# Summing the inverse steps' products in float32, wider layernorm statistics, integer table angles, and a new instruction order in a one-core Hyena-style convolution and gMLP kernel

## The chip, the core and the metric

One core of a Trainium2 chip runs the whole kernel. The time is the device time of one execution in microseconds; lower is better. Engines are named as in the profile: PE (TensorE matmul), PEld (its weight loads), DVE (VectorE), ACT (ScalarE), POOL (GpSimd) and SP (SyncE, which issues most DMAs).

## What is computed

The reference, cut to what matters (S = 2048, D = 640, F = 1728, batch 1, bfloat16 in and out):

```python
mod = (_silu(c) @ w_mod).reshape(1, 6, 1, -1)
sa, ca, ga, sb, cb, gb = ...
h = _layernorm(x) * (1 + ca) + sa
x = x + ga * _A_ref(h, A_k, A_v, A_shift_k, A_ssm_k, A_ssm_D)
h = _layernorm(x) * (1 + cb) + sb
x = x + gb * _B_ref(h, B_w_in, B_w_sp, B_b_sp, B_w_out)

def _A_ref(q, k, v, shift_k, ssm_k, ssm_D):
    kv = short_conv4(k, shift_k) * v
    y = irfft(rfft(pad(kv)) * rfft(pad(ssm_k)))[:S]      # along S
    return q * (y + kv * ssm_D)

def _B_ref(x, w_in, w_sp, b_sp, w_out):
    z = _gelu(x @ w_in)
    z1, z2 = z[..., :Fh], _layernorm(z[..., Fh:])
    g = einsum('ts,bsf->btf', w_sp, z2) + b_sp
    return (z1 * g) @ w_out
```

## The kernel before

The kernel has three stages, and one list of numbered operations covers the first two.

**The convolution stage** makes the long convolution by a Fourier transform that is written as matmuls. The 640 channels are cut into 5 units of 128 channels. For each unit, a short convolution on PE (`taps`) and a product with v on DVE (`tv`) give kv, which goes through DRAM and comes back in another layout (`kvw`, `ldX`). For the filter K and for kv (U) alike, `stage1` makes 4 groups of 4 matmuls, each evicted by `s1c`; then 8 forward steps (`forward`, 6 matmuls each) give the transform in 2 blocks of frequencies per step. A step of K is kept as bfloat16 by ACT (`khc`, the tile KH). A step of U is handled by `u_item`: DVE multiplies the real and imaginary parts from PSUM with KH, four products at a time (`prod`, 1024 elements per partition); PE transforms back (`inv`), and `zc` evicts the result into the unit's tile Z. There are 5 x 8 = 40 such items. `MODE` gives each a letter. With `u` the four products are stored in bfloat16 (tag T) and PE sums them as it transforms: 12 matmuls per item. With `s` the products are stored in float32 (tag Tf); two operations `csum` on POOL or DVE (256 elements each) form the real and imaginary sums (tile W), and PE needs 6 matmuls. Before, each unit has the letters `susussus`: 25 items are summed, 15 are not. Units 0 to 3 turn Z by a DMA transpose (`zt`) and finish with `y` on PE and `ym` on DVE; unit 4 turns on PE (`zfl`, `zk`, `yl`, `yml`). `ghm` multiplies and adds the modulation vectors, and `res` adds each unit to x.

**Tables.** The transform's cosines are made at the start (`m2_base`, `m2_chunk`): angles in float32 turns, reduced by adding and subtracting a large constant (`turns`, `msub`, on DVE), then a sine on ACT (`msin`). `msgn`, `mneg`, `gcopy` and `gneg` fill the signed and transposed copies M2 and G2.

**Statistics of the second layernorm.** In `resid`, DVE takes `bn_stats` (`ln2`) of each 128-row tile of x in three pieces: units 0 and 1 together (256 channels), units 2 and 3 together (256), and unit 4 (128). `ag2` joins the pieces, `rstd2` on POOL and `nmr2` on DVE make scale and shift, and `zx` normalises.

**The z stage** works in 4 groups of 4 row tiles. Group 0 is turned on PE (`hfl`, `hmod`); groups 1 to 3 are turned by a DMA transpose (`turn`) and modulated in place (`hmod2` on DVE, ACT or POOL). Then 16 products with `w_in` per group (`zz`, 5 matmuls of 432 columns each), `gelu` on ACT, statistics of the z2 half (`stz`, `agz`, `rstdz`, `nmrz`) and its normalisation (`zn`).

**The last stage** mixes along the sequence and projects out, both with a blocked product of 7 multiplications instead of 8 (lines 1012 and 1178). It is written out by hand, and is not touched by the change.

**What sets the order.** `ORDER` is a list of engine letters with operation numbers, written out in full; `Plan.run` issues the operations in that order, and each engine works through its own in that order. So every move between engines and every change of place is in that list. `FILLS` gives the counts of matmuls of 512 columns on a constant tile (`fill`), which compute nothing that is used; before there are three, all near the start. `SLOTS` gives the number of buffers for each tag.

Lines in the profile: L244 is the matmul helper of the first two stages, L247 the copy helper (`s1c`, `khc`, `zc`, `zk`, `gcopy`), L461 `prod`, L475 `csum`, L342 `turns`, L344 `msub`, L347 `msin`, L352 `msgn`, L607 and L609 `xn`, L660 `ghm`, L677 `ym`, L697 `res`, L703 `ln2`, L745 `yml`, L828 `ag2`, L832 `nmr2`, L844 `zx` on POOL, L857 `hfl`, L870 `hmod`, L888 `turn`, L896 `hmod2`, L925 `stz`.

Of the kernel before, what the change touches and what calls it, by code (L numbers as in the profile page):

```python
# [21 lines left out]
MAGIC = 12582912.0  # L22
# [11 lines left out]
FILLS = (9, 3, 6, )  # L34
MODE = ('susussus', 'susussus', 'susussus', 'susussus', 'susussus')
SLOTS = dict(Tf=2, W=2, X=3, X1=4, KH=9, T=3, Z=3, ZT=1, wm=1, big=2, dg=2, st1=2, s1=1, sm=2, pu=2, pz=2)
# [4 lines left out]
D0 G101 S524 D100 D102 S19 D103 S82 S2 A4 G5 S20 D121 A1 D104 D18 D109 D13 D14 P1032 P7 A105 S83 D110 D127 G6 A531 D10  # L41
S21 D15 A16 P1033 P8 D23 D11 A106 A112 S22 A111 D86 S88 D122 P26 D17 D115 A532 D87 A123 S523 D36 A533 D116 P145 A124 S3
A118 P24 P154 A117 A146 D147 D125 D27 D25 G119 A155 P1034 P151 D107 S34 D113 G126 P30 D153 G114 D31 A156 A152 G120 P28
P148 A534 A149 P133 D29 D90 D150 A134 P227 A108 P142 P161 D527 S32 P136 S33 A162 S35 D143 D528 P167 S84 P157 A228 A168
S85 P233 P171 A158 P139 P159 A234 D137 A172 P39 S526 D529 A128 D140 D530 P41 A160 P229 P163 D535 D40 A164 G536 S46 P43
G141 P173 A230 D42 P182 G48 A174 D44 D537 D184 P37 A175 A183 P179 P176 P9 A181 P231 A177 D38 P169 D178 P165 D180 S45
A170 G138 G135 P185 D542 G144 A166 D186 P195 A549 D196 G187 A232 P49 G188 A12 G553 S47 P201 P53 P211 D202 A543 G197
D212 P189 G198 S89 P217 D218 P203 P235 S525 G130 A544 A190 A204 G213 D54 P199 P205 P251 A236 G214 P191 D50 G72 G554
A252 S91 S565 P219 S58 P253 D206 A220 P249 A250 D192 A254 D200 P51 P239 D538 P221 A240 P193 D555 G131 G207 P257 A545
D222 D52 A258 D539 D540 S59 P247 A248 P215 P55 P255 P568 A256 A569 P245 D56 D541 D93 A246 P237 A238 G223 D546 G60 G224  # L50
G208 P566 A567 A550 G547 S57 P259 P265 P301 D260 D551 P61 D194 P241 D548 S570 A302 A216 P307 G557 P209 D266 A308 S92
P67 A242 P305 S94 A306 G561 P291 D68 D62 D292 P295 G562 P225 P303 D296 P573 G558 A556 G261 P243 D574 P571 S575 A559
# [30 lines left out]
D897 D1009 S1041 D1002 A993 D962 D965 P944 D991 P1024 A945 D1059 D1050 D987 S1040 D963 A898 A1025 A964 P1018 P958 D896  # L83
D994 P948 D995 A1019 D988 P1020 G1026 P1067 D1063 A959 D1027 A1021 D1057 D1029 A1028 D1060 D1061 P1012 A1030 D1031
D1064 P1069 A1013 A1068 D1062 D1058 P1071 D1072 D1065 A1070 A949 P1078 D1066 P1074 D1075 D1043 P1073 D1079 D1076 P1010
P1022 P1080 P1016 A1011 S1077 D1081 A1023 A1017 S1082
"""


# [39 lines left out]
def kernel(  # L129
# [80 lines left out]
    with ExitStack() as pctx:  # L210
# [482 lines left out]
        def resid(u, g, ns):  # L693
# [5 lines left out]
            if u not in (1, 3, 4):  # L699
                return  # L700
# [602 lines left out]
```

## Time and profile before

| | us |
|---|---|
| median of 3 runs | 307.67 |
| lowest and highest of them | 307.53, 308.72 |
| the profiled execution, its own time | 308.43 |
| its span, from first to last instruction | 306.6 |
| PE busy | 294.8 |
| DVE busy | 272.8 |
| ACT busy | 162.0 |
| POOL busy | 140.8 |

The span holds 6479 instructions at a mean granted TensorE clock of 0.988. Busy times are averages over stages with different limits, so they are read stage by stage. A matmul counts as busy from its issue to its modelled end, and matmuls overlap; the time that a series holds PE is read from the chain of waits, not from the mean duration of one. A group's busy time divided by its count leaves out the overlap of neighbours on DVE, so it lies a little below the mean duration shown beside it.

### The profile page before, as it was taken

The numbers are of one execution on the slowest core, as the hardware profiler recorded it, in microseconds if no ns is written. First come the engines' busy times: TensorE is split into PE (matmuls) and PEld (weight loads), VectorE is DVE, ScalarE is ACT, GpSimd is POOL, SyncE is SP. The second block draws the span as 40 slices with busy tenths as digits, with TensorE's granted clock in tenths as the row PEclk, the third lists the DMA queues.
The fourth block names the chain that finished last, engine by engine and source line by source line (L and its number), as shares of the span: only waits on it lengthen the run. The fifth ranks groups of instructions, "written<-read, shape, count | busy, mean of one in ns | idle before, by whom it ended". The sixth has DMA issues, their size and how long they took to land.

```text
span 306.6 us, 6479 instructions
## 1 busy us (share of the span) xinstructions
PE 294.8 (96%) x2482; PEld 195.9 (64%) x2482; DVE 272.8 (89%) x567; ACT 162.0 (53%) x287; POOL 140.8 (46%) x175
## 2 busy tenths in 40 slices
PE   6899999999999999799999999999999999999996
PEld 2476787888799888655555455555555656565554
DVE  7998999999999999979848999989989889898675
ACT  5996989998578855557656758320211111021110
POOL 2217858659796878782627231000513214040412
PEclk9799999999999999979999999999999999999999
DMA  8999999999483969205897930036758594630324
GB/s 180 227 263 249 248 255 273 227 223 238 136 203 79 219 194 274 71 3 101 199 135 169 162 53 0 0 62 137 143 116 191 80 181 91 164 81 21 83 45 123
DMA packets 127955, 45.23 MB, mean 148 GB/s; under 512 B 117071, under 2 KB 127156, under 8 KB 127924
## 3 DMA queue, kind: packets, MB, share of 16 engines
q1 hardware_dynamic: 127770, 44.78, 67.0%
q8 instruction: 19, 0.31, 0.4%
q14 instruction: 12, 0.10, 0.1%
q10 hardware_dynamic: 154, 0.05, 0.1%
HBM read 16.11 MB, written 5.24 MB: 70 GB/s over the span
## 4 chain that ended last, share of the span: by engine, by line
PE 76%; DVE 14%; DMA 4%; issue 2%; POOL 1%; ACT 1%; SPq 1%; DVEq 0%; POOLq 0%
PE ps L1012 22%; PE pu L244 17%; PE pz L244 13%; PE po L1178 7%; PE sm L244 7%; PE s L244 4%; DMA ZT<-Z 3%; PE pz L1012 2%; DVE Tf L461 2%; DMA KH<-in_A_ssm_D_dram 2%; DVE stz L925 1%; PE pu L1012 1%; DVE gh L677 1%; PE po L1139 1%; DVE st L703 1%
## 5 line engine op out<-in xcount | busy, mean ns | idle before, releaser
L244 PEld LDWEIGHTS <-Z 128*128 128x128 bf16 x320 | 31.5, 99 | 29.3 <-issue 2.2
L244 PE MATMUL pu<-X,M 128*128 128x128 bf16 (+1 forms) x480 | 45.8, 237 | 0.7 <-ACT KH L247 0.2
L1199 POOL TENSOR_TENSOR O<-O,xt 128x320 f32<-128x320 f32 x7 | 6.6, 946 | 84.8 <-ACT O L1198 84.8
L244 PEld LDWEIGHTS <-M 128*128 128x128 bf16 x480 | 37.8, 98 | 6.2 <-issue 1.5
L1012 PEld LDWEIGHTS <-S 128*128 128x128 bf16 x256 | 25.0, 98 | 21.2
L475 POOL TENSOR_TENSOR W<-Tf 128x256 bf16<-128x256 f32 x44 | 32.0, 744 | 13.4 <-DVE Tf L461 8.0
L244 PE MATMUL pu<-big,Z 128*128 128x432 bf16 x160 | 34.4, 358 | 0.9 <-DVE Z L896 0.8
L247 ACT CAST X<-s 128x1024 bf16<-128x1024 f32 x31 | 31.5, 1017 | 7.0 <-PE s L244 6.9
L244 PE MATMUL pz<-big,Z 128*128 128x432 bf16 x160 | 32.9, 347 | 0.0
L1196 ACT COPY O<-po 128x320 f32<-128x320 f32 x7 | 3.0, 425 | 52.9 <-PE po L1178 52.9
L461 DVE TENSOR_TENSOR Tf<-pu,KH 128x1024 f32<-128x1024 f32 x25 | 30.2, 1216 | 0.6 <-ACT KH L247 0.4
L1012 PEld LDWEIGHTS <-wT 128*128 128x128 bf16 x192 | 18.8, 98 | 15.8
L247 ACT CAST KH<-pu 128x512 bf16<-128x512 f32 x40 | 23.3, 598 | 6.6 <-PE pu L244 5.3
L244 PEld LDWEIGHTS <-G 128*128 128x128 bf16 x330 | 24.7, 98 | 2.0 <-issue 0.2
L247 ACT CAST Z<-pz 128x512 bf16<-128x512 f32 x35 | 20.1, 596 | 6.1 <-PE pz L244 6.0
L1012 PE MATMUL ps<-T,S 128*128 128x432 bf16 x112 | 22.7, 346 | 0.0
L1012 PE MATMUL ps<-X,wT 128*128 128x432 bf16 x112 | 22.7, 346 | 0.0
L244 PEld LDWEIGHTS <-X 128*128 128x128 bf16 x288 | 18.3, 97 | 5.8 <-issue 1.2
L1012 PE MATMUL ps<-X,S 128*128 128x432 bf16 x112 | 21.6, 346 | 0.0
L244 PE MATMUL sm<-big,dg 128*128 128x512 bf16 (+1 forms) x80 | 21.5, 398 | 0.0
L244 PE MATMUL s<-F1bd,X 128*128 128x256 bf16 x128 | 19.2, 273 | 0.5 <-DVE X L247 0.5
L925 DVE BATCH_NORM_STATS2 stz<-X 128x6 f32<-128x432 bf16 x32 | 17.9, 587 | 0.8 <-ACT X L919 0.7
(203 smaller groups left out, 628.1 us busy)
## 6 DMA issues: line engine op xcount, KB each, us to landing
wm<-in_w_mod_dram SPq DMA_DIRECT2D x6, 800.0 KB, 5.8
xt<-in_A_q_dram SPq DMA_DIRECT2D x4, 640.0 KB, 6.3
out_dram<-ot SPq DMA_DIRECT2D x15, 160.0 KB, 1.9
big<-in_B_w_in_dram SPq DMA_DIRECT2D x2, 1080.0 KB, 8.0
X<-in_A_ssm_k_dram SPq DMA_DIRECT2D x4, 512.0 KB, 6.5
kv_scr<-big SPq DMA_DIRECT2D x4, 512.0 KB, 3.0
X<-kv_scr SPq DMA_DIRECT2D x4, 512.0 KB, 4.6
w_o<-in_B_w_out_dram SPq DMA_DIRECT2D x6, 160.0 KB, 3.1
```

The costliest lines, as they stand in the source:

```text
L244: nc.tensor.matmul(o, lhsT=w, rhs=x, start=start, stop=stop)
L247: (e.copy if e is nc.scalar else e.tensor_copy)(dst, src)
L461: e.tensor_tensor(T_[:], (tl[pu] if src is None else tl[src])[:, :, :, None, :].to_broadcast(shape), tl[KH][:, :, None, :, :].to_broadcast ...
L475: e.tensor_tensor(tl[W][:, :, o, :], T_[:, :, 0, o, :], T_[:, :, 1, 1 - o, :], op=ALU.add if o else ALU.subtract)
L677: op("D", "ym", lambda e: e.tensor_tensor(ghv, ghv, src(), op=ALU.mult), r=[py], w=gk)
L703: op("D", "ln2", lambda e, n=n: e.bn_stats(out=st2[:, n, (0, 0, 0, 1, 2)[u], :], in_=xt[:, n, us[0] * DU:(u + 1) * DU]), r=[("xt", (v, n)) ...
L925: op("D", "stz", lambda e, i=i, n=n, fc=fc: e.bn_stats(out=stz[:, n, fc, :], in_=tl[z2][:, i, fc * FC:(fc + 1) * FC]), r=[(z2, (i, fc))], ...
L1012: nc.tensor.matmul(ps[:, :FC], lhsT=lhs[:, s_, :], rhs=rhs(s_), start=(s_ == 0 and not more), stop=(s_ == HT - 1), skip_group_check=more)
L1139: nc.tensor.matmul(ps[:, :hi - lo], lhsT=uTs[t][:fsz[ft], ft, :], rhs=w_o[:fsz[ft], ft, lo:hi], start=(ft == 0), stop=(ft == NFT - 1))
L1178: nc.tensor.matmul(ps[:, :HS], lhsT=w(k), rhs=x(k), start=start and k == 0, stop=stop and k == n - 1, skip_group_check=True)
L1196: nc.scalar.copy(m1, a[:, :HS])
L1199: nc.gpsimd.tensor_tensor(m5, m5, x_of(1, 1), op=ALU.add)
```

## The change

Five things change together:

- All 40 items are summed: `MODE` is `ssssssss` for each unit. That makes 15 more pairs of `csum` and 15 x 6 fewer matmuls. The slots for float32 products go from 2 to 3, those for sums from 2 to 4; the tag T is gone.
- The second layernorm's statistics of units 0 to 3 are taken in one `bn_stats` of 512 channels after unit 3 (`ln2a`), and unit 4's as before. In groups 2 and 3 ACT may take them instead, as a sum and a sum of squares, which `ln2f` on DVE then brings into the form that `bn_aggr` reads. In the new list 14 tiles are on DVE and 2 on ACT.
- The tables' angles are formed as integers, reduced with a bitwise and (`mand`), and one `msin` of 512 elements makes what two of 256 made.
- A fourth `fill` is added, and the counts go from 9, 3, 6 to 7, 5, 3, 6. The last one stands in the list ahead of the z stage's first transposes.
- `ORDER` is new as a whole. Operations that move from one engine to another, counted in the two lists (before, after):

| operation | DVE | POOL | ACT |
|---|---|---|---|
| `csum` | 6, 8 | 44, 72 | |
| `ghm` | 22, 29 | 18, 11 | |
| `res` | 10, 12 | 11, 9 | |
| `xn` | 3, 0 | 8, 9 | 5, 7 |
| `zc` | 5, 2 | | 35, 38 |
| `s1c` | 7, 5 | | 41, 43 |
| `hmod2` | 5, 8 | 8, 1 | 2, 6 |
| `zn` | 9, 8 | | 7, 8 |
| `ln2`, `ln2a` | 48, 30 | | 0, 2 |

```diff
-FILLS = (9, 3, 6, )
-MODE = ('susussus', 'susussus', 'susussus', 'susussus', 'susussus')
-SLOTS = dict(Tf=2, W=2, X=3, X1=4, KH=9, T=3, Z=3, ...)
+LN2_ACT = (2, 3)
+FILLS = (7, 5, 3, 6, )
+MODE = ('ssssssss', 'ssssssss', 'ssssssss', 'ssssssss', 'ssssssss')
+SLOTS = dict(Tf=3, W=4, X=3, X1=4, KH=9, Z=3, ...)
...
-            def turns(e):
-                new(a, "T", [P, 2, KCH, QH], F32)
-                for h in range(2):
-                    e.tensor_scalar(tl[a][:, h], tl["mbase"][:], mstep[:, h * NCH + i:h * NCH + i + 1], MAGIC, op0=ALU.add, op1=ALU.add)
-            op("DG", "turns", turns, ...)
-            op("D", "msub", lambda e: e.scalar_tensor_tensor(tl[a][:], tl[a][:], MAGIC, tl["mbase"][:, None].to_broadcast([P, 2, KCH, QH]), ...
-            for h, o in ((0, 2), (1, 0)):
-                op("A", "msin", ...)
+            op("D", "turns", lambda e: e.tensor_scalar(new(a, "Tf", [P, 2, KCH, QH], I32)[:], tl["mbase"][:], mstep[:, i:i + 1], None, op0=ALU.add), ...)
+            op("D", "mand", lambda e: e.tensor_scalar(tl[a][:], tl[a][:], 8191, None, op0=ALU.bitwise_and), w=[a])
+            op("A", "msin", lambda e: e.activation(both[:, :, :, 0:QH], tl[a][:], ACT.Sin, bias=mpi[:], scale=TWO_PI / 8192.0), ...)
...
-            if u not in (1, 3, 4):
+            if u < 3:
                 return
-            us = range(u - (u < 4), u + 1)
+            us = range(0 if u == 3 else 4, u + 1)
             for n in ns:
-                op("D", "ln2", lambda e, n=n: e.bn_stats(out=st2[:, n, (0, 0, 0, 1, 2)[u], :], in_=xt[:, n, us[0] * DU:(u + 1) * DU]), ...)
+                def stats(e, n=n, cs=cs):
+                    if e is nc.scalar:
+                        on_act2.append(n)
+                        e.activation(gh[:, n, cs], xt[:, n, cs], ACT.Copy, accum_out=sums2[:, n, 0:1])
+                        e.activation(gh[:, n, cs], xt[:, n, cs], ACT.Square, accum_out=sums2[:, n, 1:2])
+                    else:
+                        e.bn_stats(out=st2[:, n, u - 3, :], in_=xt[:, n, cs])
+                op("DA" if u == 3 and g in LN2_ACT else "D", "ln2a" if u == 3 else "ln2", stats, ...)
+            if u == 3 and g in LN2_ACT:
+                def finish(e):
...
+                op("D", "ln2f", finish, w=[("st2", (u, n)) for n in ns])
```

More of the change, by code (lines that the diff above doesn't have):

```diff
@@ L87 @@
+S1095
 """
@@ L265 @@
         NCH = NKC // KCH
-        mstep, mturn = small("mstep", 2 * NCH), small("mturn", 2 * NCH)
+        mstep = small("mstep", NCH)
         nc.vector.memset(warm[:], 0.0)
@@ L320, in m2_base @@
         def m2_base():
-            def steps(e):
-                e.tensor_scalar(mstep[:, 0:NCH], fidx[:, 0:NCH], pidx[:, 0:1], 4.0 * KCH / 8192.0, op0=ALU.mult, op1=ALU.mult)
-                e.tensor_scalar(mstep[:, NCH:], mstep[:, 0:NCH], 0.25, None, op0=ALU.add)
-                e.tensor_scalar(mturn[:], mstep[:], TWO_PI, None, op0=ALU.mult)
-            op("D", "mstep", steps, w=["mstep"])
-            def base(e):
-                e.iota(new("mbase", "KH", [P, KCH, QH], F32)[:], [[4, KCH], [64, QH]], base=1, channel_multiplier=0,
-                       allow_small_or_imprecise_dtypes=True)
-            op("G", "mbi", base, w=["mbase"], new=[("mbase", "KH")])
-            op("D", "mbase", lambda e: e.tensor_scalar(tl["mbase"][:], tl["mbase"][:], pidx[:, 0:1], 1.0 / 8192.0,
-                                                       op0=ALU.mult, op1=ALU.mult), w=["mbase"])
+            op("D", "mstep", lambda e: e.tensor_scalar(mstep[:], fidx[:, 0:NCH], pidx[:, 0:1], 4.0 * KCH, op0=ALU.mult, op1=ALU.mult),
+               w=["mstep"])
+            op("G", "mbi", lambda e: e.iota(new("mbi", "KH", [P, KCH, QH], F32)[:], [[4, KCH], [64, QH]], base=1, channel_multiplier=0,
+                                            allow_small_or_imprecise_dtypes=True), w=["mbi"], new=[("mbi", "KH")])
+            def base(e):
+                new("mbase", "Tf", [P, 2, KCH, QH], F32)
+                for h in range(2):
+                    e.tensor_scalar(tl["mbase"][:, h], tl["mbi"][:], pidx[:, 0:1], 6144.0 - 2048.0 * h, op0=ALU.mult, op1=ALU.add)
+            op("D", "mbase", base, r=["mbi"], w=["mbase"], new=[("mbase", "Tf")])
         def m2_chunk(i):
@@ L336, in m2_chunk @@
             ks = slice(i * KCH, (i + 1) * KCH)
[L339 to L349 removed]
+            op("D", "turns", lambda e: e.tensor_scalar(new(a, "Tf", [P, 2, KCH, QH], I32)[:], tl["mbase"][:], mstep[:, i:i + 1], None,
+                                                      op0=ALU.add), r=["mbase", "mstep"], w=[a], new=[(a, "Tf")])
+            op("D", "mand", lambda e: e.tensor_scalar(tl[a][:], tl[a][:], 8191, None, op0=ALU.bitwise_and), w=[a])
             both = M2[:, 0:3:2, ks, :]
+            op("A", "msin", lambda e: e.activation(both[:, :, :, 0:QH], tl[a][:], ACT.Sin, bias=mpi[:], scale=TWO_PI / 8192.0),
+               r=[a, "silut"], w=[("M2", (2, i)), ("M2", (0, i))])
             op("DG", "msgn", lambda e: e.tensor_scalar(both[:, :, :, QH:], both[:, :, :, 0:QH], sgn[:, 0:1], 1.0,
@@ L828, in norm_piece @@
                 op("D", "ag2", lambda e, n=n: e.bn_aggr(out=mv2[:, n, :], in_=st2[:, n, :, :]),
-                   r=[("st2", (u, n)) for u in (1, 3, 4)], w=[("mv2", n)])
+                   r=[("st2", (u, n)) for u in (3, 4)], w=[("mv2", n)])
             gs = slice(ns[0], ns[-1] + 1)
```

122 lines of the change are left out of this document (63 added, 59 removed).

## The prediction

> **What bounds the kernel now.** I read the page first, then busy time by stretches, the chain of waits, the groups with shapes kept apart, and the timeline. The page's first line:
>
> ```profile
> span 306.6 us, 6479 instructions
> ```
>
> The launch around that span is 1.83 us (the profiled execution took 308.43); its time lies 0.76 above the 307.67 median of the runs shown. I make the sum against 308.43 and give the forecast against the median, by the same difference. Busy time by stretches (columns: length; busy PE, PEld, DVE, ACT, POOL with counts; granted clock; DMA share; GB/s):
>
> ```profile
> 0.00:23.00 23.00, 19.08 (x127) 10.81 (x128) 20.57 (x66) 19.31 (x41) 4.86 (x18) 0.93 1.04 223
> 23.00:65.80 42.80, 42.53 (x422) 33.59 (x421) 40.46 (x76) 37.58 (x66) 31.42 (x38) 1.00 1.06 246
> 65.80:83.20 17.40, 16.79 (x208) 14.10 (x206) 17.29 (x28) 13.76 (x21) 14.44 (x15) 1.00 0.86 200
> 83.20:129.05 45.85, 44.05 (x700) 39.98 (x699) 44.29 (x73) 30.92 (x49) 35.83 (x40) 1.00 0.72 177
> 129.05:131.52 2.47, 1.37 (x42) 1.37 (x43) 2.41 (x10) 1.78 (x4) 2.30 (x3) 1.00 0.00 0
> 131.52:160.40 28.88, 28.80 (x161) 15.20 (x158) 22.07 (x76) 18.28 (x36) 13.64 (x18) 0.94 0.60 110
> 160.40:175.30 14.90, 14.06 (x77) 7.24 (x75) 13.61 (x31) 9.76 (x20) 8.67 (x10) 1.00 0.92 172
> 175.30:203.90 28.60, 28.60 (x157) 15.37 (x158) 26.43 (x59) 16.23 (x28) 3.81 (x6) 1.00 0.12 21
> ```
>
> Up to 129.05, where the first normalisation's `nmr2` ends, DVE is busy 20.57+40.46+17.29+44.29 = 122.61 us of 129.05: it idles 6.44 us. PE stands at nearly full too, so two engines are tight. The chain of waits (start, us, what) tells who ends last:
>
> ```profile
> 35.65 0.88 PE pz L244 x12
> ...
> 36.98 0.44 PE pz L244 x6
> ...
> 129.39 0.59 DVE gh L745
> ...
> 131.94 3.42 PE pu L244 x9
> ...
> 137.80 0.91 PE pu L244 x5
> ...
> 174.65 0.60 DVE Z L896
> 175.30 2.00 PE pu L244 x10
> ```
>
> A 12-matmul inverse step on `pz` holds PE 0.88 us, a 6-matmul one 0.44. At the end of the convolution it is DVE that ends last (129.39, `yml`), then the second part's first big products run from 131.5. Nine of them take 3.42 us, where five later take 0.91 (nine: 1.64): the granted clock is down, which costs 1.78. Then PE runs on with small stalls, one of them behind DVE's `hmod2` (174.65) before PE's piece at 175.30. From 203.9 on nothing is touched but the start time. So the question is how much earlier PE's product stage begins, and whether it then runs through.
>
> **The inverse steps.** Fifteen of 40 items change from unsummed to summed.
>
> ```profile
> L461 DVE TENSOR_TENSOR Tf<-pu,KH 128x1024 f32<-128x1024 f32 x25 | 30.2, 1216 | 0.6 <-ACT KH L247 0.4
> ```
>
> ```profile
> L461 DVE TENSOR_TENSOR T<-pu,KH 128x1024 bf16<-128x1024 f32 x15 | 18.2, 1216 | 0.3 <-PE pu L244 0.2
> ```
>
> DVE's product costs the same in both forms (30.2/25 = 18.2/15 = 1.21 us, f32 or bf16 out): nothing there. PE saves 15 x 0.44 = 6.6 us. In exchange there are 30 more sums, of which the new order puts 28 on POOL and 2 on DVE.
>
> **Second layernorm's statistics.** Up to `nmr2(0.0)` the old order has 13 statistics of 256 elements on DVE, the new one 2 of 512 (the rest come later in both).
>
> ```profile
> L925 DVE BATCH_NORM_STATS2 stz<-X 128x6 f32<-128x432 bf16 x32 | 17.9, 587 | 0.8 <-ACT X L919 0.7
> ```
>
> ```profile
> L703 DVE BATCH_NORM_STATS2 st<-xt 128x6 f32<-128x256 bf16 x32 | 12.3, 409 | 0.1
> ...
> L579 DVE BATCH_NORM_STATS2 st<-xt 128x6 f32<-128x320 bf16 x18 | 7.8, 477 | 0.0
> ```
>
> Busy over count: 256 elements 0.384 us, 320 0.433, 432 0.559; no row has 512. By the last two's slope (0.0011 us per element) it is 0.65, an estimate; bounds 0.56 and 0.77 (two of 256). DVE: -13 x 0.384 + 2 x 0.65 = -3.7 us. Over the kernel it is 32 x 0.384 = 12.3 against 14 x 0.65 = 9.1, with 2 tiles on ACT, whose two passes hide there in its idle time of the z stage (18.28 busy of 28.88 from 131.52 on; without that cover they hold back `gelu` by some 3 us), and two short `ln2f` on DVE, the bound's own engine.
>
> **Table angles.** Old: 8 operations of 256 and 4 of 512; new: 4 integer `turns` and 4 `mand` of 512 elements. One half more of `mbase` and two tiny `mstep` fewer cancel.
>
> ```profile
> L344 DVE SCALAR_TENSOR_TENSOR T<-T,KH 128x512 f32<-128x512 f32 x4 | 2.7, 683 | 0.0
> ...
> L342 DVE TENSOR_SCALAR T<-KH,mstep 128x256 f32<-128x256 f32 x8 | 2.4, 346 | 0.0
> ```
>
> Old: 2.4+2.7 = 5.1. The trace has no integer operation of 512. Between 0.30 (as the 256) and 0.683 (as the two-operand 512), I take 0.60, twice the 256, since the length should count: 4.8. Net -0.3, bounds -2.7 and +0.4. They lie before 23 us, where 2.4 of DVE's idle time lies too.
>
> **What the order moves between engines, up to the same point on DVE** (counted in the two lists):
>
> ```profile
> L660 DVE TENSOR_TENSOR gh<-gh,gca_bf 128x512 bf16<-128x512 bf16 x12 | 5.5, 471 | 0.0
> ...
> L247 DVE CAST Z<-pz 128x512 bf16<-128x512 f32 x5 | 3.4, 687 | 0.4 <-PE pz L244 0.4
> ...
> L609 DVE TENSOR_SCALAR gh<-xt,mv,rstd 128x640 bf16<-128x640 bf16 x3 | 1.3, 423 | 0.0
> ...
> L247 DVE CAST X<-s 128x1024 bf16<-128x1024 f32 x1 | 1.2, 1211 | 0.0
> ```
>
> ```profile
> L475 DVE TENSOR_TENSOR W<-Tf x6: 410/416/1210, 59.4 to 109.3; 128x256 bf16<-128x256 f32 x6
> ```
>
> Onto DVE: 6 `ghm` at 5.5/12 = 0.46 (+2.7), 2 sums at the median 0.416 (+0.8), one `gneg` of 1024 as two `ghm` (+0.9), one `zk` as the 0.68 cast (+0.7), and `yml` of group 1, now ahead of `nmr2(0.0)`, as half of a product (+0.6): +5.7. Off DVE: 3 `xn` at 0.43, 3 `zc` at 0.68, one `s1c` at 1.21 and one at 0.68: -5.2. Net +0.5.
>
> DVE's sum up to `nmr2(0.0)`: -3.7-0.3+0.5 = **-3.5 us**, bounds -5.9 (tables at their best) and -2.7. PE's up to the same place: -6.6, and a fourth fill: its matmuls go from 18 to 21 of 0.22 us (below), +0.6, or -6.0, and another 0.3 for a transpose group pulled ahead. PE saves more than DVE, so DVE stays the bound and PE's surplus is not gained.
>
> **POOL** is what pays.
>
> ```profile
> 32.80:119.50 86.70, 85.28 (x1063) 73.64 (x1063) 84.01 (x130) 70.27 (x116) 67.25 (x79) 1.00 0.90 208
> ```
>
> ```profile
> L475 POOL TENSOR_TENSOR W<-Tf 128x256 bf16<-128x256 f32 x44 | 32.0, 744 | 13.4 <-DVE Tf L461 8.0 <-PE pz L244 4.3 <-PE sm L244 0.8
> ...
> L697 POOL TENSOR_TENSOR xt<-xt,gh 128x512 bf16<-128x512 bf16 x11 | 13.0, 1190 | 0.5 <-DVE gh L677 0.5
> ...
> L660 POOL TENSOR_TENSOR gh<-gh,gca_bf 128x512 bf16<-128x512 bf16 x8 | 9.6, 1202 | 2.5 <-issue 2.5
> ...
> L607 POOL TENSOR_SCALAR gh<-xt,rstd,nmr 128x640 bf16<-128x640 bf16 x8 | 6.9, 874 | 0.4 <-DVE nmr L599 0.4
> ```
>
> In the stretch with sums, POOL gets 28 x 0.727 = +20.4; 7 `ghm` fewer at 1.20 (-8.4), 4 `res` fewer at 1.18 (-4.7), one `xn` more at 0.87 (+0.9): about +8.1, from 67.25 to 75.4 us. It sums after DVE's product and ahead of PE's inverse step, behind which queue the evictions `zc` and the turn through DMA of the unit. Three f32 slots (two before) and four sum slots (two) let DVE run ahead by two items, so DVE doesn't wait at once. POOL must drop from 19.45 us of idle time to about 8 in this stretch. I expect some of that to reach DVE: +0.7 us of idle time, bounds 0 and +4. The product stage then starts 2.8 us earlier.
>
> **The rule on the shared port.** DVE's sum took 0.416 in the median and 1.21 once, just while POOL's `ghm` ran until 81.71:
>
> ```profile
> 80.56 1.15 POOL L660 TENSOR_TENSOR gh<-gh,gca_bf 128x512 bf16<-128x512 bf16 x1
> 80.79 1.21 DVE L475 TENSOR_TENSOR W<-Tf 128x256 bf16<-128x256 f32 x1
> ```
>
> In the Trainium skill, "SBUF — State Buffer", section "Who interferes with whom", DVE and GpSimd share a port pair as an exclusive lock, and a DVE operation with two SBUF inputs blocks against a GpSimd one that reads SBUF. By that rule, the trace agrees, and it speaks against the change: more sums on POOL, more `ghm` on DVE. The sum above holds it only as measured: if a `ghm` takes 0.42 unhindered, as the sum does, its mean of 0.46 is 0.04 x 22, or 1 us so far.
>
> **The z stage and the fourth fill.** The new order puts 6 fill matmuls just ahead of the first transposes, where PE idles:
>
> ```profile
> 13.32 1.30 PE s L244 x6
> ```
>
> ```profile
> 130.15 0.51 PE L857 MATMUL s<-ident,Z 128*128 128x128 bf16 x6 [1.28 <-POOL Z L844]
> ```
>
> Six fills take 1.30 us and the gap is 1.28, so they hide; if PE comes there late they delay it by up to 1.30. If they keep the clock up, the 1.78 us at half clock go. In the Trainium skill, "TensorE: Matmul & The Clock Gate", section "What's actually happening", the half clock comes after at least one idle window of some 3.4 us; by that rule the 1.28 us gap alone would not have dropped it, yet the trace shows it dropped.
>
> Either way a second limit follows. Group 3's products need group 2's turn to land, then its `hmod2`, `nmr2(3.0)`, the four normalisations, and turn 3:
>
> ```profile
> 153.31 3.08 SPq L888 DMA_TRANSPOSE Z<-Z  x1
> ...
> 160.40 0.41 DVE L896 TENSOR_SCALAR Z<-Z,cb_col,sb_col 128x512 bf16<-128x512 bf16 x1 [4.40 <-DMA Z<-Z]
> ```
>
> ```profile
> 167.02 3.01 SPq L888 DMA_TRANSPOSE Z<-Z  x1
> ```
>
> Turn 2 is issued at 153.31 and lands by 160.40; turn 3 is issued 6.6 us behind that, because POOL's three normalisations queue behind its own `hmod2` and `rstdz(0)`. In the new order the way is two `hmod2` of 0.41 on DVE, a statistic of 0.56, `nmr2` of some 0.2 and two POOL normalisations at 0.87 (as `xn`), 3.3 with hand-overs some 4.1 us instead of 6.6: group 3 is ready 2.5 earlier. But two products (2 x 0.91 = 1.8) that stood ahead of group 3 now stand behind it, still to be done, so 0.7 of that is gained, whether or not the clock holds: with a full clock PE only waits longer. I take **-0.7 us** for the stage, bounds -1.8 and +1.3 (a late fill).
>
> **Sum:** -3.5+0.7-0.7 = -3.5 us; 308.43 becomes 304.9, or **304.2** against the median.
>
> **Rivals.**
> *PE sets the end* (0.20). For: the chain up to 65.8 and from 83.2 is mostly PE. If the tables cost DVE their least, DVE saves 5.9 and PE's 5.7 counts whole, the forecast's idle growth falls away, and with 0.7 it is -6.4: 301.3. Against: DVE's 97% in 83.2 to 129.05.
> *The gain is lost to waiting* (0.17). With the sums spread out, POOL, ACT and DVE are all some 90% full, and each product waits a little for a cast of `KH` or a free slot. DVE's idle time grows by 3.5 from 6.44 to 9.9 and only the z stage's 0.7 stays: 307.0. Against: all 25 float32 products together wait 0.4 us for `KH` now.
> *POOL becomes the bound* (0.07, slower). The place is 32.8 to 119.5. If its waits for products do not shrink, 19.45 us stay, the stretch lasts 8.1 longer, and less 0.7 it is 315.1. It decides from the point where POOL still idles over 11.3 us there (86.7-75.4). For: it waits for a single product again and again; against: it was 83% busy in 65.8 to 83.2 without holding anyone.
> *The lock* (0.03, slower). If each of the 36 `ghm` and sums on DVE met half a sum of 0.36, that is 13 us where about 2 are now: +11-3.5, 315. For: the one 1.21; against: the means.
> That the change doesn't do what it says has no room here: all 40 items and their sums stand in the list.
>
> **How the numbers follow.** A measurement of this kernel can tell some 0.5%, or 1.5 us, from no change: faster means below 306.1, slower above 309.2. The forecast has 0.53; with PE's case, faster is 0.73; same is 0.17; slower 0.07+0.03 = 0.10. The range reaches from just below PE's case (300.9) to just above the lost gain (307.5) and leaves the slower cases out.
>
> **What would show it.** Right: the product group (L461 before) 40 times in one form at 1.21, inverse steps only of six matmuls at 0.44; `nmr2(0.0)` near 126, with DVE still idle some 7 us ahead of it; the first big products at 0.18 each; a stall of 1 to 3 us ahead of group 3; POOL near 75 us in its stretch. A statistic of 512 above 0.77 or integer steps above 0.68 would break DVE's terms. The forecast is wrong if DVE's idle time ahead of `nmr2(0.0)` reaches 10 us, or if POOL idles more than 11 us between its first and last sum.

## The result

The changed kernel is slower: 316.48 us median of 4 runs (315.16 to 317.39) against 308.2 us (307.53 to 309.62, 4 runs) for the kernel before, a ratio of 1.026 with a 95% interval of 1.020 to 1.031. The forecast was 304.2, with a range up to 307.5. The profiled execution took 317.39, its span 314.7. The page's busy times (share of the span, instructions):

```profile
PE 289.0 (92%) x2388; PEld 189.1 (60%) x2395; DVE 272.4 (87%) x560; ACT 171.6 (55%) x308; POOL 146.8 (47%) x186
```

PE has 5.8 us less work than before (294.8), DVE about the same (272.8), and the span is 8.1 longer. Busy time by stretches (columns as in the prediction), the first four with the cuts used there, then the way to the first big product, the products up to a stop, the stop, and the rest of the z stage:

```profile
0.00:23.00 23.00, 16.95 (x129) 10.04 (x129) 20.47 (x67) 18.66 (x38) 9.49 (x23) 1.00 1.03 196
23.00:65.80 42.80, 39.55 (x360) 29.48 (x366) 37.84 (x64) 37.48 (x67) 33.72 (x41) 1.00 1.10 246
65.80:83.20 17.40, 15.98 (x195) 13.46 (x194) 15.82 (x30) 14.32 (x23) 12.82 (x15) 1.00 1.05 233
83.20:129.05 45.85, 42.10 (x646) 37.42 (x645) 44.85 (x60) 35.02 (x57) 38.10 (x47) 1.00 0.74 178
129.05:134.13 5.08, 3.85 (x82) 2.61 (x78) 5.04 (x19) 2.25 (x4) 3.50 (x6) 1.00 0.01 3
134.13:162.20 28.07, 28.06 (x159) 15.13 (x160) 22.60 (x70) 19.59 (x41) 14.21 (x17) 1.00 0.35 81
162.20:169.03 6.83, 0.03 (x2) 0.00 (x1) 1.91 (x5) 1.99 (x4) 1.03 (x2) 0.74 1.06 179
169.03:211.90 42.87, 42.87 (x227) 22.58 (x227) 38.20 (x91) 27.39 (x48) 7.92 (x10) 0.96 0.36 68
```

Two things stand out. Up to 129.05, DVE idles 2.53+4.96+1.58+1.00 = 10.07 us (6.44 before), and PE idles 6.05+3.25+1.42+3.75 = 14.5 (6.6 before). And from 162.20 to 169.03 PE does nothing (0.03 us) and no other engine is busy for more than 2.0 us, while the DMA engines are full (share 1.06).

Four marks from the timeline cut each profile into stages: the end of the last product (`prod`), the first big product of the z stage, the first product of the last stage, and the span.

| kernel | last `prod` ends | z stage begins | last stage begins | span |
|---|---|---|---|---|
| before | 119.77 | 131.52 | 203.78 | 306.6 |
| changed | 119.66 | 133.63 | 211.88 | 314.7 |

So the convolution up to its last product takes as long as before, the tail from there to the first big product 2.2 us longer, the z stage 6.0 longer (72.26 and 78.25), and the last stage the same (102.82 both). Against the forecast, the products begin 2.1 us later instead of 2.8 sooner, and the z stage is 6.0 longer instead of 0.7 shorter.

The chain of waits of the changed kernel shows the z stage's stop from one end to the other:

```profile
152.65 0.72 ACT gh L699 x2
...
153.39 0.73 ACT gh L700 x2
...
154.19 0.34 SPq L1085
...
157.73 2.77 SPq L985
...
160.67 6.35 DMA Z<-Z
...
167.04 1.52 ACT Z L906 x2
168.56 0.42 ACT M L931
...
169.03 1.96 PE pu L246 x5
170.98 1.64 PE pz L246 x5
172.62 0.91 PE pu L246 x5
```

The reader is to see how one thing hands on to the next. ACT's second pair of statistics (tile 13; L699 and L700 write the values and their squares, which nobody needs, into `gh`) ends at 154.12. Only then does SP issue the load of `w_o` (L1085), because `w_o` is given memory that `gh` held. Behind it on SP stands a load of `wT` (L985, 2.77), and behind that turn 2, at 160.67. Its input had been ready from 154.14, when POOL's normalisations ended; before, it left at 153.31. It lands at 167.02, `hmod2` follows, and PE goes on at 169.03 after 6.8 us without work, with its first ten products at half clock (1.96 and 1.64 where five take 0.91).

### The profile page after: what moved, and what is told of

It is laid out like the page before. It is cut to its first block, busy times and chain, and to the rows that moved or that the text cites. A ratio compares the mean times of both kernels' runs of the same rounds, so it can differ in the third digit from the quotient of the medians.

```text
span 314.7 us, 6334 instructions
## 1 busy us (share of the span) xinstructions
PE 289.0 (92%) x2388; PEld 189.1 (60%) x2395; DVE 272.4 (87%) x560; ACT 171.6 (55%) x308; POOL 146.8 (47%) x186
## 4 chain that ended last, share of the span: by engine, by line
PE 50%; DMA 2%; SPq 2%; DVE 2%; ACT 1%; issue 1%; DVEq 0%; ACTq 0%
PE ps L1024 22%; PE pu L246 8%; PE pz L246 8%; PE po L1190 7%; DMA Z<-Z 2%; PE pz L1024 2%; PE pu L1024 1%; PE po L1151 1%; SPq L1085 1%; SPq L985 1%; ACT Z L906 0%; DVE c L1057 0%; ACT Z L854 0%; DVE Z L882 0%; ACT gh L700 0%
## 5 line engine op out<-in xcount | busy, mean ns | idle before, releaser
L466 POOL TENSOR_TENSOR W<-Tf 128x256 bf16<-128x256 f32 x72 | 53.6, 768 | 14.0 <-DVE Tf L452 8.4
L452 DVE TENSOR_TENSOR Tf<-pu,KH 128x1024 f32<-128x1024 f32 x40 | 47.4, 1214 | 1.2 <-PE pu L246 0.8
L249 ACT CAST X<-s 128x1024 bf16<-128x1024 f32 x32 | 32.9, 1028 | 4.6 <-PE s L246 4.5
L246 PE MATMUL pz<-big,Z 128*128 128x432 bf16 x160 | 34.1, 352 | 0.2 <-DVE Z L882 0.2
L249 ACT CAST Z<-pz 128x512 bf16<-128x512 f32 x38 | 22.3, 603 | 5.2 <-PE pz L246 5.1
L246 PE MATMUL pz<-W,G 128*128 128x128 bf16 (+1 forms) x240 | 23.6, 237 | 1.2 <-DVE W L466 1.1
L246 PE MATMUL sm<-big,dg 128*128 128x512 bf16 (+3 forms) x73 | 19.4, 379 | 5.0 <-DMA big<-in_A_k_dram 2.5
L246 PEld LDWEIGHTS <-G 128*128 128x128 bf16 x240 | 18.6, 98 | 3.0 <-ACT Z L249 1.2
```

The source lines that it names most:

```text
L246: nc.tensor.matmul(o, lhsT=w, rhs=x, start=start, stop=stop)
L249: (e.copy if e is nc.scalar else e.tensor_copy)(dst, src)
L452: e.tensor_tensor(T_[:], (tl[pu] if src is None else tl[src])[:, :, :, None, :].to_broadcast(shape), tl[KH][:, :, None, :, :].to_broadcast ...
L466: e.tensor_tensor(tl[W][:, :, o, :], T_[:, :, 0, o, :], T_[:, :, 1, 1 - o, :], op=ALU.add if o else ALU.subtract)
```

## The experiments

Each profile gave the same four marks. The runs were made on four chips; a ratio compares with runs of the kernel before on the same chip, so ratios are compared below rather than times where the chips differ.

| kernel | last `prod` ends | z stage begins | last stage begins | span | ratio to before, interval |
|---|---|---|---|---|---|
| e1_ln2_dve | 120.77 | 133.87 | 203.62 | 306.5 | 1.001 (0.998 to 1.004) |
| e2_scratch | 120.44 | 133.55 | 203.22 | 306.1 | 0.999 (0.995 to 1.002) |
| e3_wo_late | 119.12 | 132.21 | 204.92 | 307.8 | 1.006 (1.003 to 1.010) |
| e4_loads | 120.84 | 134.82 | 212.52 | 315.4 | 1.031 (1.025 to 1.037) |
| e5_halfsums | 119.16 | 132.16 | 201.84 | 304.7 | 1.001 (0.997 to 1.005) |
| e6_nofill | 119.69 | 133.36 | 204.55 | 307.4 | 1.004 (1.000 to 1.007) |
| e7_oldorder | 135.66 | 150.12 | 220.31 | 323.2 | 1.054 (1.048 to 1.060) |
| e8_lessload | 121.93 | 135.04 | 204.71 | 307.7 | 1.006 (1.002 to 1.010) |
| e9_tables | 121.15 | 132.91 | 203.97 | 307.1 | 1.005 (1.002 to 1.009) |
| e10_ln2wide | 120.97 | 133.78 | 205.49 | 308.4 | 1.008 (1.004 to 1.012) |
| e11_parts | 120.72 | 133.53 | 203.85 | 306.7 | 1.002 (0.999 to 1.005) |
| e12_fill | 122.29 | 134.12 | 203.91 | 306.8 | 0.998 (0.994 to 1.001) |
| e13_lesspe | 117.74 | 130.53 | 200.42 | 303.3 | 0.995 (0.991 to 0.998) |
| e14_lessboth | 117.76 | 131.04 | 202.23 | 305.1 | 0.999 (0.995 to 1.002) |
| e16_tail | 118.90 | 132.04 | 201.72 | 304.6 | 0.999 (0.995 to 1.002) |
| e17_actq | 118.46 | 131.61 | 201.29 | 304.1 | 0.998 (0.995 to 1.002) |

One warning on reading it: the kernel before and e12 have the same instructions up to the last product, and their profiles put it at 119.77 and 122.29. A single pair of profiles says nothing about 2 us there. The tail behind it is steadier (9.28 from last `prod` to the end of `nmr2` in both).

### What holds the z stage

e1 gives ACT's two statistics (tiles 8 and 13) to DVE:

```diff
-... G658 D808 A708 D765 D712 ...
+... G658 D808 D708 D765 D712 ...
-... P872 D819 A715 D917 D767 ...
+... P872 D819 D715 D917 D767 ...
```

> The changed kernel with one edit: the two half statistics of the second layernorm that ScalarE does for token tiles 8 and 13 (each a Copy and a Square with a running sum, into the buffer gh as a throw-away target) are done by VectorE's bn_stats instead. Theory A: those passes, late on ScalarE, keep gh's memory in use; the load of w_o goes into that memory, waits for them at the head of SyncE's list, and turn(2) stands behind it, so the z stage waits. Then w_o is issued some 9 us earlier, near 145, turn(2) leaves near 154 as soon as its input is there (160.67 in the changed kernel), the 6.8 us wait of TensorE for group 2's products shrinks to under 1.5, and the time is about 309 (7 to 7.5 less than 316.5). Theory B (rival): the z stage is late because ScalarE's list is 3 us longer and DMA is slow there, whoever holds the queue: then freeing ScalarE gives at most its 3 us, 313 to 314. VectorE gets 2 x 0.65 us more, in a stretch in which it waits.

e2 leaves them on ACT and gives them another throw-away target:

```diff
+                        if "sq" not in tl:
+                            new("sq", "s1", [P, S1C, 2 * NJ * 4], F32)
+                        sq = tl["sq"][:].rearrange("p a b -> p (a b)")[:, 0:512]
-                        e.activation(gh[:, n, cs], xt[:, n, cs], ACT.Copy, accum_out=sums2[:, n, 0:1])
-                        e.activation(gh[:, n, cs], xt[:, n, cs], ACT.Square, accum_out=sums2[:, n, 1:2])
+                        e.activation(sq, xt[:, n, cs], ACT.Copy, accum_out=sums2[:, n, 0:1])
+                        e.activation(sq, xt[:, n, cs], ACT.Square, accum_out=sums2[:, n, 1:2])
```

> The changed kernel with one edit: ScalarE keeps the two half statistics, but writes their throw-away output to a PSUM tile of its own and not into gh. Nothing else moves; ScalarE's list is as long as in the changed kernel. Theory A (the memory of gh holds the load of w_o, and that load holds SyncE's list with turn(2) behind it): as good as moving the statistics to VectorE, about 309; w_o issued near 145, turn(2) near 154. Theory B (ScalarE's length or slow DMA): no change, 315 or more, and turn(2) still near 160.

e3 moves the load of `w_o` (S1055) in the list to just behind turn 2 (S922).

> The changed kernel with one edit: the load of w_o stands in SyncE's list just behind turn(2) instead of five steps ahead of it. Theory A: turn(2) no longer waits for the memory of gh and leaves near 154; the w_o load then follows it at 7 issues of half a us, and what was behind turn(2) in the list (the next loads of the weights of the last stage) comes some 3 us later; the time 310 to 313. Theory B: no change, 315 or more.

Measured: 308.27, 308.26 and 309.85 us, so theory A holds in all three (e3 comes out slightly better than its 310 to 313) and theory B falls. e2 is the sharpest, since ACT's list is as long as in the changed kernel. Its timeline of SP:

```profile
142.03 3.07 SPq L903 DMA_TRANSPOSE Z<-Z  x1
145.20 3.70 SPq L1088 DMA_DIRECT2D w_o<-in_B_w_out_dram  x7
148.96 3.12 SPq L988 DMA_TRANSPOSE wT<-in_B_w_sp_dram  x1
154.08 3.02 SPq L903 DMA_TRANSPOSE Z<-Z  x1
```

The load leaves 9 us sooner (145.20 for 154.19) and turn 2 6.6 us sooner, as soon as its input is there. The z stage takes 69.67 us instead of 78.25. In e3 the load comes behind turn 2, and what it pushes back shows: DVE waits 3.7 us for a `wT`, PE 1.8 behind a `gelu`; the z stage is 72.71.

e6 takes the fourth filling out of e2:

```diff
-FILLS = (7, 5, 3, 6, )
+FILLS = (7, 5, 3, )
```

> The kernel of the scratch experiment without the fourth group of filling matmuls (six of 512 columns on TensorE just ahead of the first products). If these keep the granted clock, the first nine or ten products run at 0.34 to 0.36 each in place of 0.18, and the time rises by 1.6 to 1.8 us, to about 310. If the clock would have held anyway, or the products are not the bound there, the time stays at 308.3 within 0.5.

It took 308.32. Its ratio lies 0.5% over that of e2, but the intervals overlap; the profiles are clearer. The first products of e6, then of e2 (start, us):

```profile
133.36 2.08 PE L246 MATMUL pz<-big,Z 128*128 128x432 bf16 x5
135.24 3.04 PE L246 MATMUL pu<-big,Z 128*128 128x432 bf16 x10
```

```profile
129.46 1.46 PE L246 MATMUL s<-ident 128*128 128x512 bf16 x6
...
134.05 0.91 PE L246 MATMUL pz<-big,Z 128*128 128x432 bf16 x4 [0.16 <-DVE Z L885]
134.79 1.99 PE L246 MATMUL pu<-big,Z 128*128 128x432 bf16 x10
```

Ten products take 3.04 us without the filling and 1.99 with it (granted clock 0.58 from 133.36 to 138.10 in e6, 1.00 from 133.55 to 138.00 in e2), and the z stage 71.19 and 69.67: in this pair the filling is worth 1.5 us. e12, the filling alone on the kernel before, has a z stage of 69.79 for 72.26, while its time leaves the gain open (306.48 us; the interval holds 1). The gain isn't the same in every profile: e13 (below) has no such filling, its first ten products take 2.70, and its z stage is 69.89.

> The kernel before with the fourth filling alone: six matmuls of 512 columns on TensorE ahead of the transposes for the first products. In the kernel before the first nine or ten products ran at half the granted clock (3.42 us); with the filling 1.64 are expected, as in the changed kernel. Theory C: the products are on the path, and the time falls by 1.5 to 1.8 us (ratio 0.994 to 0.996). Theory N: what follows them waits for other things (the layernorm of the next tiles), and the time stays within 0.3%.

### What sets the last product

e4 puts the loads of unit 1's k (S34) and v (S35) where the kernel before had them, ahead of the writes of unit 0's signal (S33, S32) and of its loads (S84).

> The changed kernel with one edit to SyncE's list: the first load of the second unit's k taps goes ahead of two weight loads, and the first load of its v taps ahead of the loads of X for unit 0, as in the kernel before. Theory L1: in the changed kernel TensorE and VectorE wait for these loads between 20 and 25 and between 35 and 45 us (2.55, 1.36 and 1.45 us for in_A_k and in_A_v), and this is why the product stage starts at 134.1 and not near 129. With the loads early 2 to 3 us of it come back: the stage starts at 131 to 132 and the time is 313.5 to 315. Theory L2 (rival): the first stretch is paced by the sums on GpSimd and the balance of the pipeline; then holes close here and open later, the stage still starts at 134 and the time stays at 316 to 317.

It took 318.47, so the one move brings nothing: PE's wait for `in_A_k` goes, and one of 1.7 us for unit 0's own signal (`kv_scr`) comes in its place, as SP's transpose now takes 6.06 us to issue and the writes leave at 17.14 for 14.51.

e5 takes 11.5 us of sums off POOL, and e8 1.3 MB off the loads, both on e2:

```diff
+                    if o and st in (1, 3, 6):
+                        return
                     e.tensor_tensor(tl[W][:, :, o, :], ...)
```

> The kernel of the scratch experiment (statistics on ScalarE with a target of their own), and of the 15 steps that the change gave float32 sums only the first of the two GpSimd sums is done; the inverse uses it twice, so the second sum's result is left out of the computation. GpSimd loses 15 x 0.77 = 11.5 us ahead of the product stage, nothing else moves. Theory P: GpSimd's sums hold the inverse steps, and that is why the product stage starts at 134 and not near 129; then it starts 2 to 3 us earlier and the time is 305 to 306. Theory L: VectorE's list sets the start, with the holes that the early loads leave in it between 20 and 45 us; then nothing changes: start 133.5 to 134.5, time 308 within 0.8.

```diff
-            op("S", "ldx", lambda e: e.dma_start(xt[:, ns, :], x_nat[:, ns, :]),
+            op("S" if h < 2 else "G", "ldx", lambda e: e.dma_start(xt[:, ns, :], x_nat[:, ns, :]) if h < 2 else e.memset(xt[:, ns, :], 0.5),
```

> The kernel of the scratch experiment, with the load of q for the upper eight token tiles left out (2 x 640 KB; GpSimd writes a constant there instead, so their rows are not the reference's). At the 240 GB/s that the DMA engines move between 20 and 45 us this is 5.3 us of their time. Theory L1: the DMA engines are full there and VectorE's holes (4.0 us between 20 and 45 in the scratch experiment) come from that; they shrink to under 2, the product stage starts 2 to 4 us earlier than 134 and the time is 304.5 to 306.5. Theory L2: the holes come from the order in which SyncE and VectorE serve the units and not from the amount; the start stays within 1 us of 134 and the time at 307.5 to 309.

e5 took 308.39: POOL's sums aren't the bound (theory P falls); POOL now idles 21.7 us ahead of its sums, and nothing is gained. e8 took 309.32, and it doesn't decide between L1 and L2, for two reasons. The loads left out were issued at 25.52 and 30.65 in e2, behind the hole at 21 to 24 us. And the constant that GpSimd writes in their place takes POOL 2.23 us from 37.97 on, just ahead of two sums; PE waits for them:

```profile
41.62 1.04 PE L246 MATMUL pz<-W,G 128*128 128x256 bf16 x12 [2.31 <-POOL W L466]
```

DVE's wait for `in_A_v` (1.7 in e2) is gone in e8, but it waits 2.0 us for POOL's sums instead.

e9 and e10 are single parts of the change on the kernel before, e11 both with the filling. Their code is that of the change: the integer `turns` and `mand`; and `bn_stats` over units 0 to 3, on DVE only.

> The kernel before with one part of the change alone: the angles of the table as integers (one add of 512 and one bitwise and of 512 a chunk, one sine a chunk). VectorE loses about 2.1 us of work (0.48 and 0.45 an operation as measured in the changed kernel, where the forecast had 0.60), all of it ahead of the first product at 31.5 us. Theory W: VectorE then only waits that much longer for what the loads and the round trip of unit 0's signal through DRAM bring; its idle time ahead of 45 us grows from 3.4 to 5 or more, the product stage starts within 0.7 of 131.5 and the time is within 0.3% of before. Theory S: VectorE's work is all that counts; the stage starts 2 us sooner and the time falls by 2 us (ratio 0.9935).

> The kernel before with one part of the change alone: the second layernorm's statistics of four units in one operation of 512 (all on VectorE, in the place of the second half; the first half's operations are dropped). Ahead of the product stage this takes 9 operations of 0.42 us off VectorE and makes a few longer by 0.25: about 3 us, in a stretch (83 to 129 us) in which VectorE is nearly full. Theory S: the stage starts 2.5 to 3.5 sooner and the time falls by 2.5 to 3.5 us (ratio 0.989 to 0.992). Theory P: TensorE is as full there and sets the end; the start moves by less than 1 us and the time by less than 0.4%.

> The kernel before, in its own order, with three parts of the change: integer angles, statistics of four units in one operation on VectorE, and the fourth filling of six matmuls ahead of the first products; without the float32 sums and without the new order. If the parts add up: 2.1 + 3 + 1.8 us, 301 to 302 us. If the angles' part is lost to waiting and the others hold: 4.8 us less, 303 (ratio 0.983 to 0.986). If TensorE sets the end and only the filling counts: 306.

They took 309.19, 310.28 and 308.77: none is faster, e9 and e10 are slower by 0.5% and 0.8%, and theory S falls in both. In e9 the idle time came as theory W has it (5.7 us ahead of 45); in e10 theory P fits best, but neither theory had expected a loss. A part of e10's is in the tail (below); for e9's 0.5% its profile shows no place. The stretch from 45 to 110 us of the kernel before, of e10 and of e11 shows why nothing is gained (PE's busy time is the second number, DVE's the fourth):

```profile
45.00:110.00 65.00, 63.94 (x790) 55.04 (x789) 62.66 (x105) 54.77 (x85) 51.66 (x58) 1.00 0.89 207
```

```profile
45.00:110.00 65.00, 63.89 (x782) 54.77 (x781) 61.49 (x101) 55.10 (x85) 50.99 (x57) 1.00 0.95 207
```

```profile
45.00:110.00 65.00, 64.16 (x788) 55.13 (x786) 61.45 (x103) 55.36 (x85) 51.39 (x57) 1.00 0.95 209
```

PE is full in all three (1.06, 1.11 and 0.84 idle). What DVE no longer does becomes DVE's idle time: 2.34, 3.51, 3.55. So it isn't DVE that sets this stretch.

e13 and e14 then take the work off PE, in the old order:

```diff
-                    mm(p_[:, k], G2[:, 1, kc, :], T_[:, k, 1], False, False)
                     mm(p_[:, k, 1], G2[:, 2, kc, :], T_[:, k, 0, 0], False, False)
-                    mm(p_[:, k, 0], G2[:, 1, kc, :], T_[:, k, 0, 1], False, False)
-                    mm(p_[:, k, 1], G2[:, 0, kc, :], T_[:, k, 1, 0], False, False)
-                    mm(p_[:, k, 0], G2[:, 3, kc, :], T_[:, k, 1, 1], False, True)
+                    mm(p_[:, k, 0], G2[:, 1, kc, :], T_[:, k, 0, 1], False, True)
```

> The kernel before, with six of the twelve matmuls left out in each of the 15 inverse steps that have no float32 sum (the terms of the second half of the product are missing from the result). TensorE loses 15 x 0.44 = 6.6 us, as in the change, but no sum is added on GpSimd and the order is the old one. Theory P: TensorE, full from 45 to 110 us, sets the end of the products; the last one ends at 114 to 117 (119.8 and 122.3 in two runs of these instructions), the time falls by 3.5 to 6 us (ratio 0.980 to 0.989). Theory D: VectorE sets it; no change beyond 1 us. Theory L: the loads and the round trips through DRAM set it; no change either, and none in the next kernel.

> The kernel of e13 with the integer angles and the statistics of four units in one operation as well: 6.6 us less on TensorE and 5 less on VectorE, in the order of the kernel before. If the two engines are the bound in turn (each covers the other's gain alone), the last product ends at 115 to 117 here, while it moved by less than 2 us with either alone; the tail is 10.25 (as with the wide statistics before), the time 303 to 305. Theory L: the last product still ends at 119 to 122 and the time stays within 1% of before.

The last product ends at 117.74 and 117.76, sooner than in all five profiles of the old order with PE's full work (119.77 to 122.29, mean 121.0), and DVE's 5 us on top change nothing. e13's time is 306.32, ratio 0.995 with an interval wholly below 1. So PE's work sets a part of this stretch before the change (theory P, but with 2.0 to 4.5 us for the 6.6 taken away, less than it expected), and what holds the rest isn't DVE. e14 took 307.23, with a tail of 10.73; its expectation of 115 to 117 and 303 to 305 failed.

e7 is the change's operations in the old order:

> The changed operations in the order of the kernel before: every queue has the list of the kernel before, with the new operations in the place of those they replace (the two sums of a step on GpSimd right behind its product, three of them for the last unit on VectorE; the half statistics of the second layernorm all on VectorE; no fourth filling). One more W buffer, and the table's base in another buffer, so that the list doesn't lock. Theory O: the new order cost the start, the operations themselves give what was forecast; then the product stage starts at 128 to 130 (131.5 before), the z stage is as before, and the time is 304.5 to 306.5. Rival: the longer sums on GpSimd hold TensorE and VectorE in this order, where a float32 step was followed by its inverse at once; then the start is at 132 or later and the time 308 to 312.

323.97 us; the rival was right, and by more than it said. PE's longest sum of waits in the stretch with sums (32 to 137 us):

```profile
PE pz L246 <- POOL W L466: 14.1, 13, 2.9
```

With a sum between product and inverse, an inverse step that follows its product at once waits for POOL. The new order is there to avoid just this, and it does: no such wait is among those of the changed kernel. What PE waits for between 20 and 121 us, before and then changed (us in total, times, longest):

```profile
PE s L244 <- DVE X L247: 0.5, 1, 0.5
PE sm L244 <- DMA ZT<-Z: 0.4, 1, 0.4
PE pu L244 <- ACT KH L247: 0.2, 1, 0.2
```

```profile
PE sm L246 <- DMA big<-in_A_k_dram: 2.5, 1, 2.5
PE s L246 <- DMA X<-kv_scr: 1.5, 2, 1.3
PE sm L246 <- DVE big L543: 1.4, 1, 1.4
PE sm L246 <- DMA ZT<-Z: 1.4, 2, 1.1
PE pu L246 <- DVE Tf L452: 0.5, 1, 0.5
PE pu L246 <- ACT KH L249: 0.3, 1, 0.3
PE s L246 <- ACT X L249: 0.3, 1, 0.3
```

1.1 us before, 7.9 after. Of these, 6.8 are loads, the signal's round trip through DRAM and the turns (`L543` waits for `in_A_v`, 1.36 at 40.17). That is about as much as the sums saved PE (6.6). But the 1.1 isn't steady: in e12, with the same instructions as the kernel before, these waits come to 4.0, while e2 in the new order has 6.9. So the new order waits more, by some 3 to 7 us. e17 tries to close the first of these holes, on top of e16 (below), by issuing unit 0's writes from ACT's queue and unit 1's k ahead of them:

```diff
-                op("S", "kvw", lambda e, sl=sl: e.dma_start(
+                op("SA" if dt == 0 else "S", "kvw", lambda e, sl=sl: e.dma_start(
```

> The kernel of e16 with the two writes of unit 0's signal to DRAM issued by ScalarE, and the load of the next unit's k ahead of the place where SyncE waited for them. Theory L (SyncE's queue, with transposes of 3 to 6 us to issue, is what the first stage waits for): TensorE's and VectorE's holes between 20 and 45 us (3.5 to 4) shrink to 2, the last product ends 1.5 to 2 us sooner than in e16, time 304.5 to 305.5. Rival: the transposes fill the DMA engines' rings whoever issues the rest, and unit 0's round trip takes as long; then as e16.

PE's wait for `in_A_k` is gone, its waits fall from 6.7 (e16) to 5.4, and PE and DVE are 1.5 and 1.7 us busier between 20 and 45. But the last product ends only 0.44 sooner, and the time (307.0, ratio 0.998; e16 0.999) is the same. Closing the first hole isn't enough.

### The tail

e16 makes four moves in e2 behind the last product: `csum` 4.4.1 (D528) ahead of an `ym` (D690), `zk` 2 (732) from DVE to ACT, `res` 1.0 (655) from DVE to POOL and there to just behind `res` 2.0 (G676).

> The kernel of the scratch experiment with four moves in the tail behind the last product: the last step's second sum ahead of an output product on VectorE, one copy of the last unit (zk 2) to ScalarE and one residual sum (unit 1, group 0) to GpSimd, both as in the kernel before or near it. VectorE's list between the last product and nmr2 loses 0.68 + 0.77 us, and the last inverse comes 1 us sooner. Expected: tail 9.2 to 9.6 in place of 10.67, product stage 1 to 1.5 us sooner, time 306.5 to 307 where the scratch kernel and the kernel before stand at 308 (ratio to before 0.994 to 0.997). If TensorE's chain or the order of the sums sets the tail, it stays at 10.5 and the time at 308.

307.63, and the tail stays at 10.71: the expectation failed. DVE's list is 1.45 us shorter, but DVE now waits (0.65, 0.22 and 0.32), so another chain sets the tail. Two of its links can be read. The `bn_stats` are one: in e10, with nothing else changed in the tail, and in e11, with only the filling besides, it grows from 9.28 to 10.25. The old order had taken units 0 and 1 early, in DVE's spare time; the statistic of 512 can start only after unit 3's residual, at the end. The other is the residual sum, in the changed kernel on DVE and POOL:

```profile
127.40 1.29 DVE L688 TENSOR_TENSOR xt<-xt,gh 128x256 bf16<-128x256 bf16 x1
```

```profile
127.39 1.16 POOL L688 TENSOR_TENSOR xt<-xt,gh 128x512 bf16<-128x512 bf16 x1
```

DVE's 256 elements take 1.29 us while POOL's sum runs, and end just after it; before, the same operation took 0.28 (126.71). The rule on the shared port (the Trainium skill, "SBUF — State Buffer", section "Who interferes with whom") fits this, as it did the 1.21 us of the prediction.

The changed kernel's own tail is 11.54 us, 0.87 more than the 10.67 of e1 and e2. Its last sum on DVE (`csum`) took 1.43 us from 120.65 on, while POOL's residual sums ran, and the same sum in e2 took 0.41 (121.39). So of the 2.2 us that the tail grew, the wide statistic's late start accounts for 1.0 (by e10) and the slow sum for about 0.9; the remaining 0.4 is not traced.

No version here that computes the whole result is faster than the kernel before by more than the measurement can tell (e13, which is, leaves out products). e1, e2, e16 and e17 win back all that the changed kernel lost.

## Why the prediction was wrong

**The step that failed** is in the sum for the statistics: that the two passes on ACT "hide there in its idle time of the z stage". Of ACT's time this is right. What was priced was the engine's time (at worst some 3 us of held-back `gelu`); not looked at was where the passes write, who gets that memory next, and what is queued behind that one. The passes take 1.5 us a tile; the wait they cause and the half clock behind it cost 8.6 us of z stage (78.25 less 69.67 in e2, whose only difference is the target). The links could be read in advance: the target `gh` in the diff, the closing of `gh`'s pool ahead of the last stage's buffers in the code, the order `ldwo`, `ldwt`, `turn` in SP's list, and turn 2 at 153.31 in a fence of the prediction.

**DVE as the bound of the first stage** failed too. DVE's busy time of 95% and its place at the end (`yml`, `nmr2`) were taken for the bound of the whole 129 us. The rival "PE sets the end" (0.20) had the argument against it: the chain of waits is mostly PE up to 65.8 and from 83.2 on. PE's waits, 1.1 us between 20 and 121, would have strengthened it. What the runs showed: DVE's work taken away before the products or between them gains nothing (e9, e10, e11, e14), and PE's 6.6 us taken away gain 2.0 to 4.5 (e13). The rival's own time, 301.3, was far off too: in the new order PE waits for loads.

**The terms, one by one**, up to the end of `nmr2(0.0)`, which came at 131.20 instead of near 126:

```profile
L466 POOL TENSOR_TENSOR W<-Tf 128x256 bf16<-128x256 f32 x72 | 53.6, 768 | 14.0 <-DVE Tf L452 8.4 <-PE pz L246 4.5 <-DVE gsa_bf L641 0.7
L452 DVE TENSOR_TENSOR Tf<-pu,KH 128x1024 f32<-128x1024 f32 x40 | 47.4, 1214 | 1.2 <-PE pu L246 0.8 <-issue 0.2 <-DVE gh L668 0.2
...
L702 DVE BATCH_NORM_STATS2 st<-xt 128x6 f32<-128x512 bf16 x14 | 9.3, 674 | 0.0
...
L337 DVE TENSOR_SCALAR Tf<-Tf,mstep 128x512 int32<-128x512 f32 x4 | 1.9, 482 | 0.3 <-ACT M L341 0.2
L339 DVE TENSOR_SCALAR Tf<-Tf 128x512 int32<-128x512 int32 x4 | 1.8, 448 | 0.1
```

- Products: 47.4/40 = 1.19 us in one form, as forecast.
- Statistics: 9.3/14 = 0.66 for the 512 (0.65 forecast). The work term of -3.7 holds; its place on the path, the tail, was not seen (+1.0 there, from e10).
- Tables: 1.9+1.8 = 3.7 us for 5.1, or -1.4 (-0.3 forecast; 0.47 an operation, not 0.60). It gained nothing: e9.
- Moves between engines: DVE's work is 131.20-10.07 = 121.1 us (122.6 before), or -1.5 (-3.5 forecast); with -3.7 and -1.4 from the two lines above, +3.6 is left in place of +0.5. The difference is operations of unchanged form that take longer, some 3.2 us over the groups that both profiles have; 2.0 of it are five residual sums like the one above. The prediction's sum held such waits "only as measured", and its rival of the lock, at +11, put them far too high.
- DVE's idle time: 10.07, where the prediction put 7.1 and named 10 as what would prove it wrong. This is the rival "the gain is lost to waiting" (9.9, 307.0) for the first stage; but the waits are for loads, not for KH or slots.
- POOL: 72.9 us in its stretch (75.4 forecast), sums at 0.768 each. It idles 13.8 us there, more than the 11 named as a sign of being wrong and the 11.3 from which it should have been the bound, and it isn't (e5). An idle time alone doesn't decide that.
- z stage without the stop: 69.67 for 72.26, -2.6 (-0.7 forecast). "With a full clock PE only waits longer" was wrong: PE is busy in all of it.

What stays open: why the last product ends at 118.5 to 121.9 in the changed order, with less work on PE and DVE, with POOL's lowered too (e5) and with single loads moved. The waits name loads and round trips, no single cure moved it by more than the profiles scatter, and no experiment removed them together.

## What to carry to other kernels

A throw-away output is a write like any other: ask which memory it keeps in use, who takes that memory next, and what is queued behind that one. Before work is taken off an engine that is 95% busy, read the waits of the others, and in more than one profile: an engine that hardly waits is the first candidate for the bound, and savings on the rest can become idle time, as here. A wider operation that can start only with its last input moves work from spare time to the end of the path.

## What the hardware showed unexpectedly

- Integer operations of 512 elements on DVE are cheap: an add with conversion 0.482 us, a bitwise and 0.448, where a float32 one with two operands took 0.683.
- After a stop of 6.8 us the first ten products ran at 1.96 and 1.64 for five (0.91 at full clock). In the Trainium skill, "TensorE: Matmul & The Clock Gate", section "What's actually happening", at least one idle window of some 3.4 us comes ahead of the half clock: the trace agrees here. At the start of the z stage the clock is low without such a window: PE's gap there is 1.28 us in the kernel before and 2.57 in e6. With six matmuls of 512 columns ahead it stayed up (1.00 in e2).
